# Splitting the direct f tiles into open, close and other halves, with eight single PSUM banks, in a gated bilinear feed-forward kernel on one Trainium2 core

## The chip, the cores and the metric

The kernel runs on one core of a Trainium2 chip. A core has five engines that run side by side, each with a queue of its own in order: TensorE (PE in the profile; PEld is its weight load), VectorE (DVE), ScalarE (ACT), GpSimd (POOL) and SyncE (SP), which issues most DMAs. TensorE writes to PSUM, which has eight banks of 128 x 512 fp32; the other data lie in SBUF. The metric is the device time of one execution in microseconds, median of several runs.

## The reference

What is computed, cut to what matters here (2048 rows, width 512, F = 1376):

```python
sa, ca, ga, sb, cb, gb = (mod[:, 0], mod[:, 1], mod[:, 2], mod[:, 3], mod[:, 4], mod[:, 5])
h = _layernorm(x, axis=-1) * (1 + ca) + sa
x = x + ga * _A_ref(h, A_wq, A_wk, A_wv, A_wo, A_beta)   # 32 heads, 4 segments, memory
h = _layernorm(x, axis=-1) * (1 + cb) + sb
x = x + gb * _B_ref(h, B_w_gate, B_w_up, B_w_down)
...
g = jnp.einsum("bsd,df->bsf", x, w_gate)
u = jnp.einsum("bsd,df->bsf", x, w_up)
h = g * u
return jnp.einsum("bsf,fd->bsd", h, w_down)
```

The change concerns only the last part, from the second layernorm on.

## The kernel before

Up to about 520 us the kernel does the attention and the product with wo. Behind it stands the gated feed-forward part. The 2048 rows are four segments of 512, taken as two pairs (p = 0: segments 0 and 1, p = 1: segments 2 and 3; c is the segment within its pair). F is cut into 11 tiles of 128 columns, the last (LAST, tile 10) with 96.

Every fp32 operand is held as a high and a low piece in the format fp32r, and a product is three matmuls (high x high, low x high, high x low). `six` (L1244) issues the six matmuls of one 256-deep product. Two f tiles and two segments are multiplied together by a scheme with seven products instead of eight, whose operands are sums and differences. A `unit` (L1352) is one such scheme for the gate (g) or the up (u) weights of two f tiles: products Z, Y, X in three PSUM banks, with copies to SBUF by ScalarE (`out_of`: p5, p1, y) and sums by VectorE (`add`, L1343). Its last two products (`seven`, `four`) are run inside the next unit. A pair of units (gate, then up) gives the mids of two f tiles: `finish` (L1328) multiplies gate and up (L1339) on VectorE where up lies in PSUM and on GpSimd otherwise, and `split` (L1269) makes the pieces mH (ScalarE) and mL (VectorE).

`build` (L1206) makes the pieces of the activations: for the combined operands GpSimd forms differences (b12 - b11 and so on) in the tile t (L1221), ScalarE makes the high piece bH (L1213) and VectorE the remainder bL (L1214). It is a generator: at each `next(nb)` one step is issued.

`down` (L1302) multiplies the mids of one or two f tiles with the down weights dH, dL, three matmuls for each, into a bank from `dbank` (L1258), and VectorE adds it to the row block xa (L1314). The banks of `dbank` rotate over lq0, the first half of lk, lq1 and the second half of lk, where lk is one tile of two banks.

Of pair p = 0 the f tiles 0, 1 and LAST are plain: `direct` (L1400) forms them without the scheme. For c = 0 there are an opening product (piece 1; its result is copied to q by ScalarE, L1413) and a closing product (piece 2) in the same bank; for c = 1 there are two products Y, to which q is added. Before: open and close of tile 0; four transposes of the layernorm (`run(lg1)`); open and close of tile 1; open and close of LAST; the down products of c = 0 (tiles 0 and 1 together, four row blocks; then LAST, four); then the c = 1 products of LAST, 0 and 1. The down products of c = 1 for these tiles are put off in the list dq: eight down products, four of LAST and four of tiles 0 and 1. Of dq the main loop (`d()`) takes one at given steps of each unit; before, three are in unit 0 and five in unit 1.

The down weights of the plain tiles, dHp and dLp, lie in the slot (wh1, wl1) in which the weight pieces cwH and cwL of unit 2 are made later, so unit 2's pieces wait for the last product that reads dHp and dLp. Weights of a unit are fetched two units ahead by `prepare`: a DMA on the SP queue into cr, sums cs on GpSimd (L478 to L482), high pieces by ScalarE (L486), low ones by GpSimd (L487). For p = 1 the pieces are fetched from DRAM instead, where p = 0 has kept them.

The order of TensorE is the order of the program (`pe`). The other engines' orders are settled when the program is built, by a scheduler that simulates the engines; `pin` only binds an instruction behind the last matmul issued, in that order, without a wait on the chip.

Of the kernel before, what the change touches and what calls it, by code (L numbers as in the profile page):

```python
# [17 lines left out]
P = 128  # L18
# [39 lines left out]
def tile_kernel(ctx, tc, x, wq, wk_, wv, wo, beta, w_gate, w_up, w_down, c, w_mod, out):  # L58
# [8 lines left out]
    def close(p):  # L67
        p.__exit__(None, None, None)
# [27 lines left out]
    TAGS = {"lq0": ("lq0", 1), "lq1": ("lq1", 1), "lk": ("lk", 1), "tb": ("tb", 1), "ms0": ("ms0", 1), "ms1": ("ms1", 1), "sm": ("sm", 1)}  # L96

    def pst(shape, tag, name, dt=F32):
        tg, n = TAGS[tag]
        return psp.tile(list(shape), dt, tag=tg, name=name, bufs=n)  # L100

    nbank, nlast = [0], [0]
    btag = ["ms", "tb", "ms", "sm"]
# [1099 lines left out]
    def tmp(name):  # L1203
        return pc.tile([P, L], F32, tag="t", name=name, bufs=NT)

    def build(p):  # L1206

        def emit(j, srcs):
            pool = bc if j < 3 else pc
            hi = pool.tile([P, 2, L], F32R, tag=f"bh{j}", name=f"bH{p}_{j}", bufs=1)  # L1210
            lo = pool.tile([P, 2, L], F32R, tag=f"bl{j}", name=f"bL{p}_{j}", bufs=1)
            for k in range(2):
                act.activation(hi[:, k], srcs[k], AF.Copy)  # L1213
                vec.tensor_sub(lo[:, k], srcs[k], hi[:, k].bitcast(F32))  # L1214
            pieces[p, j] = hi, lo

        T = pc.tile([P, 2, L], F32, tag="ws1", name=f"t{p}", bufs=1)

        def comb(a, b):
            for k in range(2):  # L1220
                nc.gpsimd.tensor_sub(T[:, k], a[k], b[k])  # L1221
            return t
# [12 lines left out]
        emit(6, comb(b22, t))  # L1235
        yield
        emit(4, comb(b21, t))
        yield
        emit(7, comb(b22, b12))
        yield  # L1240

    WI = {1: 4, 2: 5, 3: 3, 4: 6, 5: 0, 6: 1, 7: 2}
# [6 lines left out]
                pe(nc.tensor.matmul(ps[0:n], a, b[:, k], start=first and c == 0, stop=last and c == 5, skip_group_check=True))  # L1249
                c += 1  # L1250

    nx, nd, dq, lkt = [0], [0], [], [None]

    def xbank(name):
        nx[0] ^= 1
        return pst((P, 512), f"ms{nx[0]}", name)

    def dbank(name):  # L1258
        i = nd[0] % 4
        nd[0] += 1  # L1260
        if i % 2 == 0:
            return pst((P, 512), f"lq{i // 2}", name)
        if i == 1:
            lkt[0] = psp.tile([P, 2, 512], F32, tag="lk", name=name, bufs=1)
        return lkt[0][:, i // 2]

    mids, wds, x1a = {}, {}, {}

# [52 lines left out]
    def d(k=1):  # L1321
        for _ in range(k):
            if dq:
                dq.pop(0)()
# [3 lines left out]
    def finish(p, nm, f, c, v, psum):  # L1328

        n = ft[f][1]  # L1330
        if nm == "g":
            if psum:
                r = tmp(f"gs{p}_{f}_{c}")
                act.activation(r[0:n], v[0:n], AF.Copy)
                v = r
            gs[p, f, c] = v
            return
        g = gs.pop((p, f, c))
        (vec if psum else nc.gpsimd).tensor_mul(g[0:n], g[0:n], v[0:n])  # L1339
        split(p, f, c, g)  # L1340

    def add(a, b, n=P):
# [5 lines left out]
    def prev(k):  # L1348
        if len(tail) > k:
            tail[k]()  # L1350
# [46 lines left out]

        tail.extend((seven, four))

    def direct(p, f, c, qs=None):  # L1400

        n = ft[f][1]

        def mm(ps, nm, r, j, first, last):
            six(ps, *plain[p, f, nm], lambda k: (2 * r + k,), n, *pieces[p, j], first, last)

        if c == 0:
            Xs = [dirbank(f"X{nm}{p}_{f}") for nm in "gu"]
            qs = qs or [tmp(f"q{nm}{p}_{f}") for nm in "gu"]
            qt[p, f] = qs  # L1410
            for X, q, nm in zip(Xs, qs, "gu"):
                mm(X, nm, 0, 1, True, True)
                act.activation(q[0:n], X[0:n], AF.Copy)  # L1413
                yield 1
            for X, nm in zip(Xs, "gu"):
                mm(X, nm, 1, 2, False, True)
                finish(p, nm, f, 0, X, True)
                yield 2
            return
        for q, nm in zip(qt[p, f], "gu"):  # L1420
            Y = dirbank(f"Y{nm}{p}_{f}")
            mm(Y, nm, 0, 5, True, False)
            yield 3
            mm(Y, nm, 1, 3, False, True)
            finish(p, nm, f, 1, add(Y, q, n), False)
            yield 4

    qt = {}
    DB = ["ms0", "ms1", "tb", "sm"]
    ndir = [2]  # L1430

    def dirbank(name):
        ndir[0] += 1
        return pst((P, 512), DB[(ndir[0] - 1) % 4], name)

    def x_unit(n):

        for st in direct(1, LAST, 0):
            yield st
            if st == 1:  # L1440
                prev(0)
                tail[0:1] = []
        for st in direct(1, LAST, 1):
            yield st
        dq.extend(lambda c=c, t=t: down(1, (LAST,), c, t) for c in (0, 1) for t in range(4))

    def prepare(n):
# [73 lines left out]
    for n in range(NU):  # L1521
        p, nm, i = units[n]
        pr = prepare(n + 2)
        if p == 0:
            keep((nm, i), [a.rearrange("p a b c -> p (a b c)") for a in wslot[n]], wkeep)
        if n == CH - 1:
            nb = build(1)
        for st in (unit if nm != "x" else x_unit)(n):
            next(pr, None)
            if n == 0:  # L1530
                next(pr1, None)
                next(nb, None)
# [12 lines left out]
    d(99)  # L1545
    close(pcpool)
    close(wppool)
    close(B["bcpool"])
# [26 lines left out]
```

## Time and profile before

| | |
|---|---|
| median of 3 runs | 898.79 us (897.49 to 901.04) |
| the profiled execution | 899.35 us |
| its span, first to last instruction | 897.6 us |
| mean granted TensorE clock | 0.990 of full speed |
| TensorE busy after 720 us, stretch 720 to 760 | 37.88 of 40 us |
| VectorE, ScalarE, GpSimd busy in the whole span | 623.5, 496.3, 426.8 us |

The profile is of one execution. A row of a timeline has the start in microseconds, the duration, the engine, the line of the kernel, the operation, output and inputs, and in brackets how long the engine stood idle before it and what released it. The view of the waits adds these up by line and releaser. The view by stretches has for each engine the busy time with the count of instructions, and PEclk, the clock that the throttle granted. A share of busy time is an average over stages with different limits, so the stretches matter more than the page.

### The profile page before, as it was taken

The numbers are of one execution on the slowest core, as the hardware profiler recorded it, in microseconds if no ns is written. First come the engines' busy times: TensorE is split into PE (matmuls) and PEld (weight loads), VectorE is DVE, ScalarE is ACT, GpSimd is POOL, SyncE is SP. The second block draws the span as 40 slices with busy tenths as digits, with TensorE's granted clock in tenths as the row PEclk, the third lists the DMA queues.
The fourth block names the chain that finished last, engine by engine and source line by source line (L and its number), as shares of the span: only waits on it lengthen the run. The fifth ranks groups of instructions, "written<-read, shape, count | busy, mean of one in ns | idle before, by whom it ended". The sixth has DMA issues, their size and how long they took to land.

```text
span 897.6 us, 14464 instructions
## 1 busy us (share of the span) xinstructions
PE 855.1 (95%) x4976; PEld 600.3 (67%) x4976; DVE 623.5 (69%) x1689; ACT 496.3 (55%) x745; POOL 426.8 (48%) x552
## 2 busy tenths in 40 slices
PE   8989999989999999999999978999999999999998
PEld 4755656556565556666666766777788768888876
DVE  7798777888788877878887366775756834444444
ACT  3758767687676865777454452333444734554420
POOL 4546536565564763756235456638771401116310
PEclk9999999999999999999999999999999999999999
DMA  7555434454554555365674474447753565443012
GB/s 235 146 160 144 115 109 135 149 150 133 132 125 142 145 151 136 109 193 168 193 223 131 153 271 166 164 138 267 264 172 133 214 208 199 177 156 119 30 47 94
DMA packets 83305, 141.29 MB, mean 157 GB/s; under 512 B 11712, under 2 KB 45504, under 8 KB 83232
## 3 DMA queue, kind: packets, MB, share of 16 engines
q1 hardware_dynamic: 83088, 140.35, 49.6%
q8 instruction: 39, 0.64, 0.3%
q14 instruction: 34, 0.28, 0.1%
q10 hardware_dynamic: 144, 0.02, 0.0%
HBM read 90.52 MB, written 49.55 MB: 156 GB/s over the span
## 4 chain that ended last, share of the span: by engine, by line
PE 72%; DVE 14%; ACT 6%; POOL 3%; DMA 2%; issue 2%; SPq 0%; POOLq 0%; ACTq 0%; DVEq 0%
PE acc L1311 12%; PE tb L85 7%; PE q L85 6%; PE k L85 6%; PE Xg L1249 6%; PE Xu L1249 6%; DVE q L39 5%; PE wops L85 4%; PE vps L85 4%; PE Yu L1249 3%; PE kps L85 3%; PE Yg L1249 3%; PE qps L85 3%; ACT pt L331 2%; PE Zu L1249 1%
## 5 line engine op out<-in xcount | busy, mean ns | idle before, releaser
L39 DVE CUSTOM_DVE_ANT_0 q<-q,cmask 128x384 f32<-128x384 f32 (+3 forms) x512 | 246.5, 508 | 49.7 <-PE q L85 39.6
L331 ACT ACTIVATE pt<-k 128x1024 f32<-128x1024 f32 x160 | 163.8, 1024 | 64.4 <-PE k L85 63.7
L337 POOL TENSOR_SCALAR_AFFINE_SELECT pt<-pt 128x256 f32<-128x256 f32 (+1 forms) x224 | 96.8, 446 | 166.8 <-ACT pt L331 163.1
L85 PE MATMUL q<-kst,qst 96*128 96x384 bf16 (+3 forms) x512 | 101.5, 299 | 11.4 <-DVE nm L39 9.8
L1314 DVE TENSOR_TENSOR xa<-xa,acc 128x512 f32<-128x512 f32 x95 | 64.9, 683 | 62.2 <-PE acc L1311 62.0
L85 PE MATMUL k<-qst,kst 98*128 98x384 bf16 (+3 forms) x512 | 97.1, 302 | 5.0 <-ACT pt L331 4.9
L85 PE MATMUL tb<-pt,v 128*32 128x512 f32 (+3 forms) x1024 | 75.5, 436 | 0.0
L39 DVE DVE_READ_ACCUMULATOR2_ANT nm<- 128x1 f32 x512 | 72.0, 141 | 0.0
L85 PEld LDWEIGHTS <-kst 98*128 98x128 bf16 x512 | 37.7, 98 | 49.5 <-issue 43.2
L85 PEld LDWEIGHTS <-qst 96*128 96x128 bf16 x512 | 43.1, 97 | 37.9 <-issue 14.0
L1311 PE MATMUL acc<-dH,mH 128*128 128x512 f32 (+1 forms) x150 | 60.1, 401 | 0.0
L1311 PE MATMUL acc<-dH,mL 128*128 128x512 f32 (+1 forms) x150 | 59.6, 398 | 0.3 <-DVE mL L1274 0.3
L1311 PE MATMUL acc<-dL,mH 128*128 128x512 f32 (+1 forms) x150 | 59.7, 398 | 0.0
L1339 POOL TENSOR_TENSOR p1g<-p1g,p1u 128x512 f32<-128x512 f32 x9 | 11.7, 1295 | 95.1 <-DVE p1u L1343 95.1
L85 PEld LDWEIGHTS tb<-pt,v 128*32 128x32 f32 x1024 | 28.7, 109 | 38.6 <-issue 34.1
L363 ACT ACTIVATE tsb<-tb 128x512 f32<-128x512 f32 x32 | 19.0, 595 | 41.0 <-PE tb L85 41.0
L1311 PEld LDWEIGHTS acc<-dH,mL 128*128 128x128 f32 (+1 forms) x150 | 28.4, 190 | 7.3 <-DVE mL L1274 0.6
L1311 PEld LDWEIGHTS acc<-dH,mH 128*128 128x128 f32 (+1 forms) x150 | 28.4, 190 | 7.2 <-ACT mH L1273 0.3
L1311 PEld LDWEIGHTS acc<-dL,mH 128*128 128x128 f32 (+1 forms) x150 | 28.5, 190 | 7.1
L85 PE MATMUL kps<-ahH,wkH 128*128 128x512 f32 x64 | 29.7, 464 | 0.6 <-DVE ahH L39 0.6
L85 PE MATMUL wops<-woH,oH 128*128 128x512 f32 x64 | 28.3, 442 | 0.7 <-ACT oH L512 0.7
L85 PE MATMUL qps<-ahH,wqH 128*128 128x512 f32 x64 | 28.7, 448 | 0.0
(384 smaller groups left out, 2174.3 us busy)
## 6 DMA issues: line engine op xcount, KB each, us to landing
wm<-in_w_mod_dram SPq DMA_DIRECT2D x24, 256.0 KB, 4.9
kd<-k SPq DMA_DIRECT2D x16, 384.0 KB, 2.5
kst<-kd SPq DMA_DIRECT2D x32, 192.0 KB, 3.2
qd<-q SPq DMA_DIRECT2D x16, 384.0 KB, 2.9
qst<-qd SPq DMA_DIRECT2D x32, 192.0 KB, 3.6
x<-in_x_dram SPq DMA_DIRECT2D x16, 256.0 KB, 4.6
kst<-kd SPq DMA_DIRECT2D x32, 128.0 KB, 3.1
qst<-qd SPq DMA_DIRECT2D x32, 128.0 KB, 3.6
```

Source lines behind the costliest of these rows:

```text
L39: i = getattr(self.eng, name)(*a, **k)
L85: return pe(nc.tensor.matmul(*a, **k))
L331: ex = act.activation(pt, kp, AF.Exp, scale=0.25)
L337: sels[u, i] = nc.gpsimd.affine_select(w, w, pattern=[[0, w.shape[1]], [1, P]], compare_op=ALU.is_ge, fill=0.0, base=0, channel_multiplier=-1)
L363: act.activation(tsbs[u], tbs.pop(u), AF.Copy)
L1249: pe(nc.tensor.matmul(ps[0:n], a, b[:, k], start=first and c == 0, stop=last and c == 5, skip_group_check=True))
L1311: pe(nc.tensor.matmul(ps, a[0:m, t * P:(t + 1) * P], b[0:m], start=j == 0, stop=j == n - 1))
L1314: vec.tensor_add(xa, xa, ps)
L1339: (vec if psum else nc.gpsimd).tensor_mul(g[0:n], g[0:n], v[0:n])
```

## The change

- The PSUM pool of the first part is closed after it, and a second pool with eight single banks is opened; lk becomes lk0 and lk1, and `dbank` rotates over lk0, lq1, lk1 and lq0.
- `direct` is divided into `open0`, `close0` and `other`. The order is now: open of tiles 0 and 1, close of tile 0, the transposes, close of tile 1, open of LAST, two down products of tiles 0 and 1, close of LAST, two more; then `other(LAST)`, two down products of LAST, `other(0)`, the two others, `other(1)`.
- In `build` the differences on GpSimd and the splits are steps of their own, the splits are pinned, and for p = 1 the order of the steps differs. In the last units of p = 0 a step is issued at every step of the unit.
- In `finish` the multiplication is always on VectorE: 31 instructions, in both pairs, leave GpSimd.
- All eight put-off down products of c = 1 are issued in unit 0.

```diff
-    psp = ctx.enter_context(tc.tile_pool(name="psp", bufs=1, space=PSUM))
+    psppool, psp = open_pool(name="psp", bufs=1, space=PSUM)
+    PS = [psp]
...
+    close(psppool)
+    psgpool, PS[0] = open_pool(name="psg", bufs=1, space=PSUM, reuse_waits="tile")
...
             for k in range(2):
-                act.activation(hi[:, k], srcs[k], AF.Copy)
-                vec.tensor_sub(lo[:, k], srcs[k], hi[:, k].bitcast(F32))
+                pin(act.activation(hi[:, k], srcs[k], AF.Copy))
+                pin(vec.tensor_sub(lo[:, k], srcs[k], hi[:, k].bitcast(F32)))
...
         if p > 0:
+            emit(2, b21)
+            yield
+        comb(b12, b11)
+        yield
+        if p > 0:
             emit(1, b11)
             yield
-            emit(2, b21)
-            yield
-        emit(5, comb(b12, b11))
+        emit(5, t)
         yield
         emit(3, b22)
         yield
-        emit(6, comb(b22, t))
-        yield
+        comb(b22, t)
+        yield
+        emit(6, t)
+        yield
...
     def dbank(name):
-        i = nd[0] % 4
         nd[0] += 1
-        if i % 2 == 0:
-            return pst((P, 512), f"lq{i // 2}", name)
-        if i == 1:
-            lkt[0] = psp.tile([P, 2, 512], F32, tag="lk", name=name, bufs=1)
-        return lkt[0][:, i // 2]
+        return pst((P, 512), ("lq0", "lk0", "lq1", "lk1")[nd[0] % 4], name)
...
-        (vec if psum else nc.gpsimd).tensor_mul(g[0:n], g[0:n], v[0:n])
+        vec.tensor_mul(g[0:n], g[0:n], v[0:n])
...
+    def dmm(p, f, ps, nm, r, j, first, last):
+        six(ps, *plain[p, f, nm], lambda k: (2 * r + k,), ft[f][1], *pieces[p, j], first, last)
+
+    def open0(p, f, qs=None):
+
+        n = ft[f][1]
+        qt[p, f] = qs or [tmp(f"q{nm}{p}_{f}") for nm in "gu"]
+        xt0[p, f] = [dirbank(f"X{nm}{p}_{f}") for nm in "gu"]
+        for X, q, nm in zip(xt0[p, f], qt[p, f], "gu"):
+            dmm(p, f, X, nm, 0, 1, True, True)
+            act.activation(q[0:n], X[0:n], AF.Copy)
+            yield 1
+
+    def close0(p, f):
+
+        for X, nm in zip(xt0.pop((p, f)), "gu"):
+            dmm(p, f, X, nm, 1, 2, False, True)
+            finish(p, nm, f, 0, X, True)
+            yield 2
...
-    run(direct(0, 0, 0, qa[0]))
+    run(open0(0, 0, qa[0]))
+    run(open0(0, 1, qa[1]))
     next(xp)
+    run(close0(0, 0))
     run(lg1)
     nb = build(0)
     next(nb)
-    run(direct(0, 1, 0, qa[1]))
+    run(close0(0, 1))
     for w in wdp[:2]:
         next(w)
+    run(open0(0, LAST, qa[LAST]))
+    next(wdp[2])
     next(nb)
     next(pr0)
-    run(direct(0, LAST, 0, qa[LAST]))
-    next(wdp[2])
-    for t in range(4):
+    for t in range(2):
+        down(0, (0, 1), 0, t)
+    next(nb)
+    run(close0(0, LAST))
+    next(nb)
+    for t in range(2, 4):
         next(pr0, None)
         down(0, (0, 1), 0, t)
...
-    for t in range(4):
-        down(0, (LAST,), 0, t)
...
-    for f in (LAST, 0, 1):
-        for _ in direct(0, f, 1):
-            if f != LAST:
-                next(pr1, None)
-        if f == LAST:
-            next(nb)
+    run(other(0, LAST))
+    next(nb)
+    next(nb)
+    for f in (0, 1):
+        for t in (2 * f, 2 * f + 1):
+            down(0, (LAST,), 0, t)
+        for _ in other(0, f):
+            next(pr1, None)
+        next(nb)
...
-            if st in DS[nm] and n < NU - 1:
+            if n == 0:
+                d(1 + st % 2 if st > 1 else 1)
+            elif st in DS[nm] and n < NU - 1:
                 d()
             if 1 <= n < CH - 1:
                 next(lg, None)
-            if n == CH - 1 and st in (1, 3, 5, 6) or n == CH:
+            if n in (CH - 1, CH):
                 next(nb, None)
```

More of the change, by code (lines that the diff above doesn't have):

```diff
@@ L94, in tile_kernel @@
     dram = ctx.enter_context(tc.tile_pool(name="dram", bufs=1, space=DRAM))
-    psp = ctx.enter_context(tc.tile_pool(name="psp", bufs=1, space=PSUM))
-    TAGS = {"lq0": ("lq0", 1), "lq1": ("lq1", 1), "lk": ("lk", 1), "tb": ("tb", 1), "ms0": ("ms0", 1), "ms1": ("ms1", 1), "sm": ("sm", 1)}
+    psppool, psp = open_pool(name="psp", bufs=1, space=PSUM)
+    PS = [psp]
+    TAGS = {"lq0": ("lq0", 1), "lq1": ("lq1", 1), "lk": ("lk", 1), "lk0": ("lk0", 1), "lk1": ("lk1", 1), "tb": ("tb", 1), "ms0": ("ms0", 1), "ms1": ("ms1", 1), "sm": ("sm", 1)}
     def pst(shape, tag, name, dt=F32):
         tg, n = TAGS[tag]
-        return psp.tile(list(shape), dt, tag=tg, name=name, bufs=n)
+        return PS[0].tile(list(shape), dt, tag=tg, name=name, bufs=n)
     nbank, nlast = [0], [0]
@@ L1221, in comb @@
                 nc.gpsimd.tensor_sub(T[:, k], a[k], b[k])
-            return t
         t = [T[:, k] for k in range(2)]
@@ L1234, in build @@
         yield
-        emit(6, comb(b22, t))
+        comb(b22, t)
         yield
-        emit(4, comb(b21, t))
+        emit(6, t)
         yield
-        emit(7, comb(b22, b12))
+        comb(b21, t)
+        yield
+        emit(4, t)
+        yield
+        comb(b22, b12)
+        yield
+        emit(7, t)
         yield
@@ L1250, in six @@
                 c += 1
-    nx, nd, dq, lkt = [0], [0], [], [None]
+    nx, nd, dq = [0], [0], []
     def xbank(name):
@@ L1398, in unit, with other @@
         tail.extend((seven, four))
-    def direct(p, f, c, qs=None):
+    def dmm(p, f, ps, nm, r, j, first, last):
+        six(ps, *plain[p, f, nm], lambda k: (2 * r + k,), ft[f][1], *pieces[p, j], first, last)
+    def open0(p, f, qs=None):
         n = ft[f][1]
[L1404 to L1419, printed above, removed]
+        qt[p, f] = qs or [tmp(f"q{nm}{p}_{f}") for nm in "gu"]
[9 more added lines that the diff above has]
+            yield 2
+    def other(p, f):
+        n = ft[f][1]
         for q, nm in zip(qt[p, f], "gu"):
             Y = dirbank(f"Y{nm}{p}_{f}")
-            mm(Y, nm, 0, 5, True, False)
+            dmm(p, f, Y, nm, 0, 5, True, False)
             yield 3
-            mm(Y, nm, 1, 3, False, True)
+            dmm(p, f, Y, nm, 1, 3, False, True)
             finish(p, nm, f, 1, add(Y, q, n), False)
             yield 4
+    xt0 = {}
     qt = {}
@@ L1436, in x_unit @@
     def x_unit(n):
-        for st in direct(1, LAST, 0):
+        for st in open0(1, LAST):
             yield st
[L1440 to L1444, printed above, removed]
+            prev(0)
+            tail[0:1] = []
+        yield from close0(1, LAST)
+        yield from other(1, LAST)
         dq.extend(lambda c=c, t=t: down(1, (LAST,), c, t) for c in (0, 1) for t in range(4))
@@ L1545, in tile_kernel @@
     d(99)
+    close(psgpool)
     close(pcpool)
```

## The prediction

> **What bounds the kernel now.** I read the page first, then the waits of TensorE in the part that the diff touches (520.4 us to the end), then the timeline around each of these waits.
>
> ```profile
> span 897.6 us, 14464 instructions
> PE 855.1 (95%) x4976; PEld 600.3 (67%) x4976; DVE 623.5 (69%) x1689; ACT 496.3 (55%) x745; POOL 426.8 (48%) x552
> PE 72%; DVE 14%; ACT 6%; POOL 3%; DMA 2%; issue 2%; SPq 0%; POOLq 0%; ACTq 0%; DVEq 0%
> ```
>
> TensorE (PE) is busy for 95% of the span and carries 72% of the chain that ended last; the diff leaves out no matmul. A gain can only be time in which PE stands still or runs slowly, a loss only a new wait of PE. These are its waits after 520.4 us (total, times, longest):
>
> ```profile
> PE Xg L1249 <- ACT q L1413: 5.4, 2, 2.7
> PE Yg L1249 <- ACT p5g L1363: 3.9, 2, 2.1
> PE Zg L1249 <- POOL cwL L487: 2.3, 1, 2.3
> ...
> PE acc L1311 <- DVE mL L1274: 0.3, 1, 0.3
> ```
>
> The timeline of PE gives their places (start, duration; the wait in brackets):
>
> ```profile
> 528.68 0.66 PE L88 MATMUL ctp<-ident,x 128*128 128x128 f32 x4 [1.29 <-ACT chf L596]
> 534.81 0.50 PE L1249 MATMUL Xg<-bh,gH 128*128 128x512 f32 x1 [2.73 <-ACT q L1413]
> 535.40 0.63 PE L1249 MATMUL Xg<-bl,gH 128*128 128x512 f32 x1
> 535.83 0.63 PE L1249 MATMUL Xg<-bh,gH 128*128 128x512 f32 x1
> ...
> 544.92 0.48 PE L1249 MATMUL Xg<-bh,cwH-1_6808 128*96 128x512 f32 x1 [2.70 <-ACT q L1413]
> ...
> 555.30 0.39 PE L1311 MATMUL acc<-dLp,mH 96*128 96x512 f32 x1
> 555.78 0.50 PE L1311 MATMUL acc<-dHp,mH 96*128 96x512 f32 x1
> ...
> 582.11 0.50 PE L1249 MATMUL Yg<-bH,cwH 128*128 128x512 f32 x1 [1.75 <-ACT p5g L1363]
> ...
> 604.38 0.49 PE L1249 MATMUL Zg<-bh,cwH 128*128 128x512 f32 x1 [0.49 <-ACT cwH L486]
> 607.17 0.79 PE L1249 MATMUL Zg<-bh,cwL 128*128 128x512 f32 x1 [2.29 <-POOL cwL L487]
> 617.74 0.39 PE L1311 MATMUL acc<-dH,mL 128*128 128x512 f32 x1
> ...
> 732.28 0.50 PE L1249 MATMUL Yg<-bH,cwH 128*128 128x512 f32 x1 [2.12 <-ACT p5g L1363]
> ```
>
> Granted clock by stretches (length; busy time and count of PE, PEld, DVE, ACT, POOL; PEclk; DMA):
>
> ```profile
> 528.00:535.00 7.00, 3.58 (x17) 2.76 (x18) 5.54 (x5) 6.37 (x12) 7.00 (x5) 1.00 1.04 369
> 535.00:545.00 10.00, 7.30 (x25) 5.13 (x24) 9.91 (x9) 4.70 (x9) 9.37 (x8) 0.83 0.36 134
> 600.00:617.00 17.00, 14.22 (x55) 11.05 (x54) 13.10 (x17) 7.10 (x13) 14.58 (x16) 0.90 0.54 201
> 617.00:650.00 33.00, 33.00 (x152) 26.64 (x150) 21.78 (x32) 14.53 (x25) 25.94 (x27) 1.00 0.78 279
> ```
>
> Without waits a matmul takes 33.00/152 = 0.22 us. After a long gap the starts lie 0.43 us apart (535.40 to 535.83), and the clock of that stretch is 0.83 or 0.90. In the timeline some 8 matmuls go so after each gap of 1.75 us and more: 8 x 0.21, about 1.6 us on top of the gap. After the gap of 1.29 us the stretch shows 1.00, so I charge none there.
>
> The Trainium skill (TensorE: Matmul & The Clock Gate, Why this matters for your kernels) advises against idle gaps above some 3 us. By it, gaps of 1.75 to 2.73 us would not have slowed the clock, and removing them would save the gaps alone; this trace has slow matmuls after each, so I go by the trace.
>
> **What is removed.** (1) The closing products of f tile 1 and of the last tile wait for the copy of their own opening products. In the new order another tile's products lie between: 2.73 + 2.70, and 1.6 after each, 8.6 us. (2) The 1.29 at the transposes is given to the same reordering; the last tile's down products lose two waits for a half of the two-bank tile (555.30 to 555.78 is 0.48, 0.25 over the usual distance; the second alike). Together 1.8. (3) In unit 0, Yg waits for p5g because ScalarE stands at mH, whose product GpSimd makes late:
>
> ```profile
> 580.42 0.63 ACT L1273 ACTIVATE mH<-q 128x512 fp32r<-128x512 f32 x1 [1.74 <-POOL q L1339]
> 581.48 0.58 ACT L1363 ACTIVATE p5g<-Yg 128x512 f32<-128x512 f32 x1
> ```
>
> Now that mul is on VectorE, and four held-back down products stand between Yg's halves: 1.75 + 1.6 = 3.4. (4) Unit 2's weights lie in the slot of the held-back down weights, which is free at the end of unit 0 instead of unit 1, so Zg finds its pieces: 0.49 + 2.29 + 1.6 = 4.4. Sum: 8.6 + 1.8 + 3.4 + 4.4 = 18.2.
>
> **What is added, at the first down product.** It needs mL of f tile 1. PE gets there so: from 534.81 take the waits 2.73 and 1.29, add 24 matmuls (closing f tile 1, opening the last tile), 536.1, and its second half about 0.7 later; say 537.0. In the built program's order ScalarE has the first copy of b12-b11 ahead of mH, VectorE its remainder ahead of mL, and GpSimd makes that difference only after cwL-1 and five instructions for the next unit's weights (three cs, two cwL):
>
> ```profile
> 526.91 2.79 POOL L435 TENSOR_TENSOR cwL-1_6809<-cr-1_6810,cwH-1_6808 128x1024 fp32r<-128x1024 f32 x1 [16.09 <-ACT cwH-1_6808 L434]
> 529.66 1.74 POOL L1221 TENSOR_TENSOR t<-chf,chf 128x512 f32<-128x512 f32 x1
> 531.36 1.18 POOL L478 TENSOR_TENSOR cs<-cr 128x256 f32<-128x256 f32 x1
> ...
> 535.32 1.73 POOL L487 TENSOR_TENSOR cwL<-cr,cwH 128x512 fp32r<-128x512 f32 x1
> ...
> 558.10 0.73 POOL L478 TENSOR_TENSOR cs<-cr 128x256 f32<-128x256 f32 x1 [7.86 <-DMA cr<-in_w_up_dram]
> ...
> 564.75 1.30 POOL L487 TENSOR_TENSOR cwL<-cr,cwH 128x512 fp32r<-128x512 f32 x1 [3.71 <-ACT cwH L486]
> ```
>
> ```profile
> 531.08 0.94 ACT L486 ACTIVATE cwH<-cr 128x512 fp32r<-128x512 f32 x2 [0.17 <-DMA cr<-in_w_gate_dram]
> 540.41 1.77 DVE L1214 TENSOR_TENSOR bL<-t,bH 128x512 fp32r<-128x512 f32 x1
> 542.70 0.68 DVE L1214 TENSOR_TENSOR bL<-t,bH 128x512 fp32r<-128x512 f32 x1
> ```
>
> The weights cr land at 531.0. Then GpSimd needs, at the short durations, 3 x 0.73 + 1.30 + 0.73 and 1.29 for the difference (by L487 of the same size): ready at 536.5. At the long ones, 3 x 1.18 + 1.73 + 1.18 + 1.74: 539.2. Behind it come the copy (0.6), one remainder at 1.77 and one at 0.68: mL at 539.5 to 542.5. PE waits 2.5 to 5.5 and pays the slow clock, 1.6: bounds 2.5 (without it) and 7.1. The stretch 535 to 545 had VectorE at 9.91 and GpSimd at 9.37 of 10, so I go toward the upper end: 5.8. Behind the stopped down product stand only PE's own products.
>
> **What is added, at the first down product of pair one (f tiles 2, 3; c = 1).** Before, it came 108 matmuls after the start of Zu of unit 1; now 81, since 27 of the held-back products are ahead. PE's cover shrinks by 27 x 0.22 = 5.9 us while VectorE gains three muls in it:
>
> ```profile
> 601.81 1.28 DVE L1289 TENSOR_TENSOR crd<-crd,gbb 128x512 f32<-128x512 f32 x2
> 611.50 0.69 DVE L1343 TENSOR_TENSOR p5u<-Xu,p5u 128x512 f32<-128x512 f32 x1 [2.96 <-PE Xu L1249]
> 612.10 2.86 DVE L587 TENSOR_SCALAR x<-x,cmv,cy 128x512 f32<-128x512 f32 x3
> 615.50 0.68 DVE L1274 TENSOR_TENSOR mL<-p5g,mH 128x512 fp32r<-128x512 f32 x1
> ```
>
> From p5u to the matmul that needs mL there are 617.74 - 611.50 = 6.2 us. By the new order eleven VectorE instructions lie there: four x at 0.95 (2.86 for three) and seven others at 0.6 (611.50 to 612.10): 8.0. That is a wait of 1.8, if no more is contended. At the far end the four with two inputs in SBUF take 1.8 instead of 0.68 (the 1.77 above), 4.3 more, and the slow clock 1.6: 7.7. The nearest rows, 601.81 to 615.50, show short durations, so I take the short wait with its slow stretch: 3.4.
>
> **At no cost.** Of the 31 muls taken from GpSimd the others stand in units where PE was always busy:
>
> ```profile
> L1339 DVE TENSOR_TENSOR gs<-gs,Xu x13: 671/678/689, 526.2 to 872.3; 128x512 f32<-128x512 f32 x11, 96x512 f32<-96x512 f32 x2
> L1339 POOL TENSOR_TENSOR p5g<-p5g,p5u x9: 1288/1292/1522, 612.3 to 869.4; 128x512 f32<-128x512 f32 x9
> ```
>
> One takes 0.68 instead of 1.29, so what follows it comes earlier unless VectorE is late; it had 11 us free of 33 in the stretch from 617. If that cover fails, rival C. The single banks add no wait; the wait at 732.28 for p5g (2.12, behind a fetched weight copy) keeps its order and stays, as does the tail.
>
> On this the Trainium skill (SBUF — State Buffer, Who interferes with whom) speaks against the change: a VectorE instruction with two SBUF inputs and a GpSimd one that reads SBUF block each other. The trace agrees that something does: 1.77 against 0.68 for the same line.
>
> Sum: -18.2 + 5.8 + 3.4 = -9.0. The profiled execution took 899.35 us (span 897.6), 0.56 above the median of 898.79. So 898.8 - 9.0 = **889.8 us**. With both added waits at their low ends (2.5, 1.8) it is 884.9, at their high ends 895.4.
>
> **Rivals.** A: no new waits, because mL comes in time at both places: 880.6. For it: the short GpSimd durations at 558. Against: the order puts the difference behind five instructions. B: both at full price, 895.4. For it: GpSimd busy for all of 528 to 535. C, slower: VectorE becomes last at the end of later pairs. PE already waits once for mL (0.3), so a delay of VectorE there shows at once. GpSimd is busy for 25.94 of 33 us in the stretch from 617; I take three pairs at such a load. Each such wait at 3 us (the size of the ones now removed) with 1.6 is 4.6; three of them and B: 895.4 + 13.8 = 909. It decides for slower from the second full wait on. Against: clock 1.00 and PE busy throughout from 617 to 650. D: the change doesn't do what it says: p5g and Zg still wait, their releaser being a fetch rather than the mul or slot: 889.8 + 3.4 + 4.4 = 897.6. By the skill's rule on gaps the slow stretches are in neither sum: -11.8 + 4.2 + 1.8 = -5.8, 893.0, which I give 0.05.
>
> **How the numbers follow.** My forecast (884.9 to 894) has 0.49, A 0.14, B 0.14, C 0.13, D 0.05, the rule 0.05. A measurement of this kernel can tell about 0.5%, 4.5 us, from no change: the forecast, A and the rule are faster (0.68), B and D the same (0.19), C slower (0.13). The range goes from A, 880.0, past D to 900.0: what is left out is C and little below A.
>
> **What would show it.** Right: no gap above 1 us in closing products; Zg of unit 2 and Yg of unit 0 without a wait; one wait of PE at the first down product for mL, one at the first of pair one; no mul of L1339's kind on GpSimd; VectorE about 20 us busier. Wrong: waits for mL in later pairs (C), no wait in the two new places (A), Yg or Zg still waiting (D), or a clock below 1.00 where PE has no gap.

## The result, and the profile after

The changed kernel takes 901.27 us (median of 20 runs, 899.39 to 903.71); the kernel before took 898.72 beside it. The ratio is 1.0033 with a 95% interval of 1.0022 to 1.0045: 2.5 us slower, where 889.8 had been forecast. The two profiled executions, 899.35 before and 900.34 after, lie 1.0 us apart, and the account below is made between these two.

TensorE's waits in the changed kernel from 520 us on (total, times, longest):

```profile
PE Xu L1260 <- DVE p5u L1349: 5.2, 3, 2.8
PE acc L1317 <- ACT mH L1279: 5.1, 2, 3.0
PE acc L1317 <- DVE mL L1280: 4.4, 2, 3.1
PE Yg L1260 <- ACT p5g L1369: 2.4, 1, 2.4
PE Xu L1260 <- DVE yu L1349: 1.2, 2, 0.9
...
```

Every wait that was to go is gone: none of the closing products, of Yg in unit 0 or of Zg in unit 2. In their place stand waits for mH and mL, forecast as one wait for mL at each of two places, and for p5u, which were not forecast. Their places, in TensorE's timeline of the changed kernel:

```profile
521.10 0.50 PE L1260 MATMUL Xg<-bh,gH 128*128 128x512 f32 x1 [0.78 <-DVE xr L39]
...
539.61 0.49 PE L1317 MATMUL acc<-dHp,mH 128*128 128x512 f32 x1 [2.11 <-ACT mH L1279]
541.35 0.50 PE L1317 MATMUL acc<-dHp,mL 128*128 128x512 f32 x1 [1.24 <-DVE mL L1280]
...
594.73 0.40 PE L1260 MATMUL Zg<-bh,cwH 128*128 128x512 f32 x1
...
604.71 0.40 PE L1317 MATMUL acc<-dH,mH 128*128 128x512 f32 x1
...
608.56 0.50 PE L1317 MATMUL acc<-dH,mH 128*128 128x512 f32 x1 [2.98 <-ACT mH L1279]
612.19 0.79 PE L1317 MATMUL acc<-dH,mL 128*128 128x512 f32 x1 [3.13 <-DVE mL L1280]
618.54 0.48 PE L1260 MATMUL Zu<-bh,cwH 128*128 128x512 f32 x1
...
646.34 0.50 PE L1260 MATMUL Xu<-bH,cwH 128*128 128x512 f32 x1 [2.81 <-DVE p5u L1349]
...
711.29 0.50 PE L1260 MATMUL Xu<-bH,cwH 128*128 128x512 f32 x1 [1.62 <-DVE p5u L1349]
...
734.79 0.50 PE L1260 MATMUL Yg<-bH,cwH 128*128 128x512 f32 x1 [2.38 <-ACT p5g L1369]
...
894.32 0.40 PE L1317 MATMUL acc<-dL,mH 128*128 128x512 f32 x1
```

And the same matmuls in the kernel before, as far as they are not shown above:

```profile
520.45 0.39 PE L1249 MATMUL Xg<-bh,gH 128*128 128x512 f32 x1
...
616.80 0.40 PE L1311 MATMUL acc<-dH,mH 128*128 128x512 f32 x1
...
621.77 0.48 PE L1249 MATMUL Zu<-bh,cwH 128*128 128x512 f32 x1
...
893.38 0.40 PE L1311 MATMUL acc<-dL,mH 128*128 128x512 f32 x1
```

The reader should subtract row from row. The part begins 0.65 us late (521.10 against 520.45). At Zg of unit 2 the changed kernel is 9.65 us ahead (594.73 against 604.38), and as Zg no longer waits, 12.09 ahead at the first matmul of pair one's first down product (604.71 against 616.80). At Zu of unit 3, right behind the next ones, it is 3.23 ahead (618.54 against 621.77): 8.9 us are gone there. The wait at 646.34 with its slow stretch takes the rest and 0.6 more, the one at 711.29 adds 1.62, and at the last matmul the changed kernel is 0.94 behind (894.32 against 893.38). The stretches show where the clock fell:

```profile
535.00:545.00 10.00, 6.65 (x22) 4.45 (x21) 8.72 (x9) 6.33 (x11) 9.38 (x8) 0.84 0.59 208
600.00:617.00 17.00, 10.10 (x34) 7.34 (x33) 14.18 (x16) 6.13 (x10) 13.26 (x13) 0.80 0.66 240
617.00:650.00 33.00, 30.19 (x131) 23.95 (x130) 23.33 (x35) 12.84 (x22) 11.12 (x13) 0.96 0.44 152
720.00:760.00 40.00, 37.62 (x163) 29.84 (x162) 17.44 (x27) 16.54 (x26) 0.00 (x0) 1.00 0.66 225
```

From 600 to 617 us TensorE ran 34 matmuls where the kernel before ran 55. What VectorE and GpSimd did there, in the changed kernel:

```profile
597.70 2.89 DVE L1295 TENSOR_TENSOR crd<-crd,gbb 128x512 f32<-128x512 f32 x1
...
601.11 0.68 DVE L1349 TENSOR_TENSOR p5u<-Xu,p5u 128x512 f32<-128x512 f32 x1
...
603.46 3.26 DVE L588 TENSOR_SCALAR x<-x,cmv,cy 128x512 f32<-128x512 f32 x3
606.63 1.21 DVE L1345 TENSOR_TENSOR p5g<-p5g,p5u 128x512 f32<-128x512 f32 x1
607.76 2.58 DVE L588 TENSOR_SCALAR x<-x,cmv,cy 128x512 f32<-128x512 f32 x1
...
611.46 0.68 DVE L1280 TENSOR_TENSOR mL<-p5g,mH 128x512 fp32r<-128x512 f32 x1
```

```profile
597.19 2.85 POOL L488 TENSOR_TENSOR cwL<-cs,cwH 128x1024 fp32r<-128x1024 f32 x1
...
607.26 2.80 POOL L488 TENSOR_TENSOR cwL<-cs,cwH 128x1024 fp32r<-128x1024 f32 x1
```

The mL that TensorE waits for (611.46) stands behind four scalings x of the next layernorm. Two of VectorE's instructions last as long as a weight piece of GpSimd that runs at the same time: crd ends at 600.59 and cwL at 600.04, x at 610.34 and cwL at 610.06.

### The profile page after: what moved, and what is told of

Read it like the earlier page. It is cut to its first block, busy times and chain, and to the rows that moved or that the text cites. A ratio compares the mean times of both kernels' runs of the same rounds, so it can differ in the third digit from the quotient of the medians.

```text
span 898.6 us, 14447 instructions
## 1 busy us (share of the span) xinstructions
PE 852.6 (95%) x4975; PEld 600.1 (67%) x4976; DVE 647.0 (72%) x1720; ACT 496.7 (55%) x745; POOL 389.3 (43%) x521
## 4 chain that ended last, share of the span: by engine, by line
PE 71%; DVE 15%; ACT 6%; DMA 2%; issue 2%; POOL 2%; SPq 1%; ACTq 0%; DVEq 0%; POOLq 0%
PE acc L1317 13%; PE tb L85 7%; PE q L85 6%; PE k L85 6%; PE Xg L1260 6%; DVE q L39 5%; PE Xu L1260 5%; PE wops L85 4%; PE vps L85 4%; PE Yg L1260 4%; PE Yu L1260 4%; PE kps L85 3%; PE qps L85 2%; ACT pt L332 2%; PE Zu L1260 1%
## 5 line engine op out<-in xcount | busy, mean ns | idle before, releaser
L479 POOL TENSOR_TENSOR cs<-cr 128x256 f32<-128x256 f32 x10 | 8.6, 856 | 107.2 <-DMA cr<-in_w_gate_dram 102.3
L488 POOL TENSOR_TENSOR cwL<-cr,cwH 128x512 fp32r<-128x512 f32 (+1 forms) x20 | 22.7, 1158 | 40.9 <-ACT cwH L487 40.9
L1260 PE MATMUL Xu<-bH,cwH 128*128 128x512 f32 (+1 forms) x68 | 27.4, 403 | 6.4 <-DVE p5u L1349 5.2
```

The lines of the kernel that those rows point to most:

```text
L479: gp.tensor_add(S[:, 0], A(1, 0), A(1, 1))
L488: gp.tensor_sub(wl[:, d], v, wh[:, d].bitcast(F32))
```

## The experiments

The names used in the expectations: M says that the gate times up products fill VectorE by themselves; Q, that it is what stands ahead of the last mL in VectorE's queue; P, that it is the cover taken out of unit 1; L, that VectorE stands still for whole GpSimd instructions; W says that the wait at the first down product hangs on the place that the difference b12 - b11 has on GpSimd, A that mL of tile 1 comes at its own time whatever GpSimd does (this A is not the prediction's rival A). Every run was timed in five rounds beside the kernel before; ratios are to that kernel, with a 95% interval. Versions that lie within some 2 us of each other have overlapping intervals; between these the text goes by the traces.

| run | median us | ratio | interval |
|---|---|---|---|
| products back on GpSimd | 893.77 | 0.9944 | 0.9923 to 0.9966 |
| put-off products spread | 894.69 | 0.9951 | 0.9934 to 0.9968 |
| scalings x four steps later | 889.26 | 0.9890 | 0.9865 to 0.9915 |
| weight pieces in quarters | 897.25 | 0.9976 | 0.9961 to 0.9992 |
| x later, difference first | 888.72 | 0.9892 | 0.9873 to 0.9911 |
| before, products on VectorE alone | 895.66 | 0.9974 | 0.9958 to 0.9989 |
| x later, difference first, products shared | 886.32 | 0.9860 | 0.9838 to 0.9883 |
| before, put-off products in unit 0 alone | 903.54 | 1.0056 | 1.0035 to 1.0078 |
| shared, last tile closed first | 885.48 | 0.9841 | 0.9818 to 0.9864 |
| the same, weight work free | 884.49 | 0.9834 | 0.9812 to 0.9857 |
| before, put-off and single banks | 900.22 | 1.0014 | 0.9994 to 1.0034 |
| x later, all products on GpSimd | 887.24 | 0.9864 | 0.9842 to 0.9885 |

### Products back on GpSimd

```diff
-        vec.tensor_mul(g[0:n], g[0:n], v[0:n])
+        (vec if psum else nc.gpsimd).tensor_mul(g[0:n], g[0:n], v[0:n])
```

> The changed kernel with one part undone: the gate times up products that come from SBUF are on GpSimd again. In the changed kernel TensorE loses 9.9 us at the first down product of pair one (waits 2.98 for mH and 3.13 for mL, then the slow clock), and 2.81 and 1.62 to p5u at 646 and 711 us. Theory M (the moved products themselves fill VectorE): both go, the wait at pair one falls under 1 us and no p5u wait is left: about 901.3 - 9.9 - 4.4 = 887. Theory Q (the queue in front of the last product counts: scalings x of the next layernorm stand ahead of mL on VectorE and are held up by GpSimd's weight pieces of 2.3 to 2.9 us): the p5u waits go, but at pair one the product now stands behind these weight pieces on GpSimd, and 3 us or more of wait stay: 891 to 897.

It took 893.77. Pair one still waits. Of the p5u waits the one of 2.81 shrinks to 0.31, and those of 0.79 and 1.62 go (0.17 stands at 752.36, where the changed kernel has none). The scalings x on VectorE, and TensorE's waits, of this run:

```profile
603.83 4.04 DVE L588 TENSOR_SCALAR x<-x,cmv,cy 128x512 f32<-128x512 f32 x4
```

```profile
609.12 0.79 PE L1317 MATMUL acc<-dH,mL 128*128 128x512 f32 x1 [3.46 <-DVE mL L1280]
...
640.17 0.50 PE L1260 MATMUL Xu<-bH,cwH 128*128 128x512 f32 x1 [0.31 <-DVE p5u L1349]
```

With no product on VectorE, four x still stand ahead of mL. So M is out for pair one, and right for the p5u waits of 2.81 and 1.62: in the changed kernel's order these need the products on VectorE.

### Put-off products spread over units 0 and 1

```diff
-            if n == 0:
-                d(1 + st % 2 if st > 1 else 1)
-            elif st in DS[nm] and n < NU - 1:
+            if st in DS[nm] and n < NU - 1:
                 d()
```

> The changed kernel with one part undone: the put-off down products of c = 1 are three in unit 0 and five in unit 1 again. Theory P (the loss at pair one comes from the 27 matmuls of cover taken out of unit 1): the waits of 6.1 us there fall under 1 us, and what comes back is the wait of Zg for unit 2's weights, 2.8 us and a slow stretch: 901.3 - 9.9 + 4.4 = 896, or lower. Theory Q: the cover of 5.9 us hides most of the 6.1 as well, so both agree on that place; by Q the p5u waits at 646 and 711 (2.81, 1.62) stay, by P, if all the loss comes from the earlier arrival of TensorE, they shrink by the time given back.

It took 894.69. No wait is left at pair one; Zg waits again, 0.49 and 1.21, and Yg 0.61 behind it, for the weight pieces. The cover is a condition of the loss, with one thing that comes with it: the slot of unit 2's weights is again free late, GpSimd's large piece starts at 609.16, behind that mL (607.68), and the four x take 3.4 (0.96, 1.93 and 0.53). Which of the two counts for more this run does not part. But the wait for p5u is the same 2.81 as in the changed kernel, though TensorE now reaches it some 5 us earlier:

```profile
641.05 0.50 PE L1260 MATMUL Xu<-bH,cwH 128*128 128x512 f32 x1 [2.81 <-DVE p5u L1349]
```

So that wait is no matter of how early TensorE comes; VectorE's chain moves with it.

### Scalings x four steps later

```diff
-            if 1 <= n < CH - 1:
+            if 1 <= n < CH - 1 and (n > 1 or st > 4):
                 next(lg, None)
```

> The changed kernel with the steps of the next layernorms (loads, statistics, scalings x, transposes) begun four steps later, so that on VectorE no scaling x stands ahead of the product p5g and of mL at the first down product of pair one. Nothing else changes. Theory Q: mL comes some 6 us earlier (three x 3.26 and one x 2.58 leave the queue), the wait at pair one falls from 6.1 to under 1.5 us, and the p5u wait at 646 us, where an x that waits 0.94 for GpSimd stands ahead, falls from 2.81 to under 1: about 889 to 893. Theory M: the same time as the changed kernel within 2 us, because the products themselves are what is late.

It took 889.26, 12.0 us less than the changed kernel with the same products, banks and order of TensorE's work, except that the transposes come later too. VectorE begins the mL that TensorE waits for at 607.57 instead of 611.46. At pair one TensorE waits 1.34 for p5u and 0.51 for mL, instead of 0.79 for p5u and 6.1 for mH and mL, and at the end of the next pair not at all. Q holds at both places.

### Weight pieces in quarters

```diff
         for d, v in ((slice(4, 6), top), (6, A(1, 1)), (slice(0, 4), S)):
             act.activation(wh[:, d], v, AF.Copy)
-            gp.tensor_sub(wl[:, d], v, wh[:, d].bitcast(F32))
+            if d == slice(0, 4):
+                for j in range(4):
+                    gp.tensor_sub(wl[:, j], S[:, j], wh[:, j].bitcast(F32))
+            else:
+                gp.tensor_sub(wl[:, d], v, wh[:, d].bitcast(F32))
```

> The changed kernel with the longest weight-piece subtraction of each unit on GpSimd (128 x 1024, 2.4 to 2.9 us) issued as four of 128 x 256. GpSimd's total work is the same or a little more. Theory L (VectorE's instructions with two inputs in SBUF, and the scalings x, stand still for a whole GpSimd instruction): the 2.89 of crd at 597.70 and the 2.58 of x at 607.76 fall to 1.3 or less, and the wait at pair one falls from 6.1 to 3 or 4 us: 895 to 898. If they share the port in turn all along, the durations add up to the same and the time stays within 1.5 us of 901.3.

It took 897.25. VectorE in this run:

```profile
597.91 1.23 DVE L1299 TENSOR_TENSOR crd<-crd,gbb 128x512 f32<-128x512 f32 x1
...
604.02 3.54 DVE L592 TENSOR_SCALAR x<-x,cmv,cy 128x512 f32<-128x512 f32 x4 [0.80 <-POOL cy L589]
```

The crd that took 2.89 takes 1.23, beside a piece of GpSimd of 1.19, and four x take 3.54 where three and one took 3.26 and 2.58. Shorter instructions of GpSimd hold VectorE up for less, as L says; by the rival, sharing in turn, the time would have stayed within 1.5 us of 901.3. TensorE still waits 4.42 for mL, where L had 3 to 4: the queue is the greater part.

### The kernel before with one part of the change

The first has the products on VectorE alone, the second all put-off products in unit 0 alone, the third the second with the eight single banks.

```diff
-        (vec if psum else nc.gpsimd).tensor_mul(g[0:n], g[0:n], v[0:n])
+        vec.tensor_mul(g[0:n], g[0:n], v[0:n])
```

> The kernel before with the gate times up products on VectorE alone, nothing else of the change. Theory Q (VectorE's chain up to p5u does not get earlier when TensorE does; before, p5u was done 0.3 us ahead of TensorE at 646): the 1.75 for p5g in unit 0 goes, Zg's wait for unit 2's weights stays (it hangs on the slot), TensorE comes to p5u at 646 and 711 earlier or VectorE later, and waits 1 to 3 us at each: 898 to 902. Theory M (VectorE with three products more in each pair is the bound by itself): a wait for mL at pair one of 2 us or more beside them: 903 or more.

It took 895.66, better than either theory had it. It has no wait at pair one, and one p5u wait:

```profile
645.52 0.50 PE L1249 MATMUL Xu<-bH,cwH 128*128 128x512 f32 x1 [2.81 <-DVE p5u L1343]
```

Again 2.81. By itself this part is a gain of 3.1 us: p5g's wait in unit 0 falls to 0.84 and Zg's second wait to 1.20.

```diff
-            if st in DS[nm] and n < NU - 1:
+            if n == 0:
+                d(1 + st % 2 if st > 1 else 1)
+            elif st in DS[nm] and n < NU - 1:
                 d()
```

> The kernel before with all eight put-off down products of c = 1 in unit 0, nothing else of the change: the products gate times up stay on GpSimd. Theory P and Q agree that Zg's wait (0.49 + 2.29 and a slow stretch, 4.4) goes. By P (the cover of 27 matmuls is what pair one lacks, whatever engine multiplies) a wait of 3 to 6 us with a slow stretch comes at the first down product of pair one: 897 to 902. By M (the products on VectorE are what is late) no wait comes there: 894.5.

It took 903.54: alone, this part is a loss of 4.8 us. Pair one waits 1.07 and 3.46, the same as with the changed kernel's products back on GpSimd. A wait that no theory had named stands in unit 0. TensorE of this run:

```profile
585.67 0.80 PE L1311 MATMUL acc<-dHp,mH 96*128 96x512 f32 x1 [4.38 <-DVE xa L1314]
```

And with the single banks too:

```diff
+    close(psppool)
+    psgpool, PS[0] = open_pool(name="psg", bufs=1, space=PSUM, reuse_waits="tile")
...
-        i = nd[0] % 4
         nd[0] += 1
-        if i % 2 == 0:
-            return pst((P, 512), f"lq{i // 2}", name)
-        if i == 1:
-            lkt[0] = psp.tile([P, 2, 512], F32, tag="lk", name=name, bufs=1)
-        return lkt[0][:, i // 2]
+        return pst((P, 512), ("lq0", "lk0", "lq1", "lk1")[nd[0] % 4], name)
```

> The kernel before with all eight put-off down products in unit 0, as in the earlier run of that part alone, which took 903.5, and with the eight single banks of the change in addition. There TensorE waited 4.38 at the second put-off product for an xa of VectorE. If that wait is for the bank (half of the two-bank tile is still read by xa), it goes with its slow stretch: 897 to 899.5, and the loss at pair one (1.07 + 3.46 and a slow stretch, products on GpSimd) stays. If VectorE is simply late there, the wait stays and the time is within 1.5 us of 903.5.

With the banks it took 900.22, 3.3 us less; the upper end of the expectation was 899.5. The wait of 4.38 is gone, though the sums xa of VectorE come as late (584.94 without the banks, 586.17 with them), so it was for the two-bank tile. It stood at the fourth put-off product, the last one of LAST, and not at the second, as the expectation says; a wait of 0.99 for xa stands at the sixth, of tiles 0 and 1 (586.90). Pair one's wait stays (3.45).

### The wait at the first down product

```diff
+        wpin = pin if n == 0 else (lambda i: i)
-        gp.tensor_add(S[:, 0], A(1, 0), A(1, 1))
+        wpin(gp.tensor_add(S[:, 0], A(1, 0), A(1, 1)))
...
-            gp.tensor_sub(wl[:, d], v, wh[:, d].bitcast(F32))
+            wpin(gp.tensor_sub(wl[:, d], v, wh[:, d].bitcast(F32)))
```

> The run before it with the scalings x begun four steps later, and with one step more: the weight sums and low pieces of unit 0 are bound behind the opening product of the last tile, so that on GpSimd the difference b12 - b11 stands right behind cwL-1 and ahead of them. Theory W (the wait at the first down product, 2.50 + 1.23 with a slow stretch, some 5 us, comes from that difference standing behind five weight instructions): the difference is made from 533.7 on, as soon as its operand is there, mL comes at 537 to 538.5, the wait falls to 1.5 or less: 884 to 887. Rival (ScalarE and VectorE are as late for reasons of their own, their copies and remainders): the wait stays at 2.5 or more and the time at 888 to 890.

This is made from the run with x later. It took 888.72, 0.5 less than without this step. GpSimd makes the difference from 533.12 on and ScalarE has copied both halves at 537.62, and still TensorE waits 1.28 for mH and 1.72 for mL, where it was 2.50 and 1.23. ScalarE's copies, then VectorE, then TensorE, of this run:

```profile
535.98 0.60 ACT L1341 ACTIVATE gs<-Xg 128x512 f32<-128x512 f32 x1
...
538.03 0.63 ACT L1280 ACTIVATE mH<-gs 128x512 fp32r<-128x512 f32 x1
```

```profile
534.93 1.31 DVE L1281 TENSOR_TENSOR mL<-gs,mH 128x512 fp32r<-128x512 f32 x1 [1.65 <-ACT mH L1280]
536.16 1.23 DVE L1298 TENSOR_TENSOR dLp<-crd,dHp 128x512 fp32r<-128x512 f32 x1
537.32 0.68 DVE L1346 TENSOR_TENSOR gs<-gs,Xu 128x512 f32<-128x512 f32 x1
...
539.12 1.75 DVE L1281 TENSOR_TENSOR mL<-gs,mH 128x512 fp32r<-128x512 f32 x1
```

```profile
540.93 0.79 PE L1318 MATMUL acc<-dHp,mL 128*128 128x512 f32 x1 [1.72 <-DVE mL L1281]
```

The product gs of tile 1 itself comes at 537.32: ScalarE has copied its gate only at 536.58, and VectorE, which stood 1.65 for tile 0's mH, does that tile's mL and a weight remainder ahead of it. W, which had a wait of 1.5 or less, falls. The difference is not without a part, though. In the changed kernel ScalarE stands 1.34 for it, and mH of tile 1, whose product has been there since 537.84, is copied only behind it:

```profile
538.41 0.63 ACT L1216 ACTIVATE bH<-t 128x512 fp32r<-128x512 f32 x1 [1.34 <-POOL t L1224]
538.95 0.61 ACT L1279 ACTIVATE mH<-gs 128x512 fp32r<-128x512 f32 x1
```

With the difference first the wait for mH is 1.2 shorter; but its remainders are then ahead of mL on VectorE, and the wait for mL is 0.5 longer.

Closing the last tile before the first two down products gives TensorE 12 matmuls more there:

```diff
-    for t in range(2):
-        down(0, (0, 1), 0, t)
     next(nb)
     run(close0(0, LAST))
+    for t in range(2):
+        down(0, (0, 1), 0, t)
     next(nb)
```

> The kernel with the shared products (x later, difference first, products of tiles 8, 9 and of p = 1 on GpSimd), with one edit: the last tile is closed before the first two down products instead of after them. There TensorE waited 1.52 for mH and 1.73 for mL and then ran slowly. Theory A (mL of tile 1 comes at its own time, some 3 us after TensorE, whatever GpSimd does, so 12 matmuls more ahead of it, 2.7 us, hide it): the two waits fall to 1 us or less, but a wait of up to 0.7 for q of the last tile comes ahead of its closing product: 2 to 4 us less, 882 to 884.5. Rival (the closing product brings its own instructions on VectorE and ScalarE ahead of mL, which then comes later by as much): within 1 us of 886.3.

It took 885.48, 0.8 less than the run it was made from (that with the products shared, below). The waits for mH and mL are gone, and the wait for q of the last tile took their place, not 0.7 but 2.85, since ScalarE has four copies of the difference and of b22 ahead of it. By its time the run lies in the rival's range, but not for the rival's reason:

```profile
539.78 0.47 PE L1261 MATMUL Xg<-bh,cwH-1_6812 128*96 128x512 f32 x1 [2.85 <-ACT q L1417]
```

Without the binding of unit 0's weight work, all else the same:

> The run before it in this set without the binding of unit 0's weight work on GpSimd: the difference b12 - b11 again stands behind five weight instructions. By the order, mH of tile 1 then stands ahead of the second piece of the difference on ScalarE. Theory W (that place on GpSimd decides when mL comes): slower than the run before it by 1.5 us or more. Theory A (it does not): within 1 us of it.

It took 884.49, 1.0 less and not 1.5 more: with the difference late again, q comes ahead of its copies on ScalarE, and the wait is 1.27 and 0.32. The difference of 1.0 is not clear of noise, but 1.5 more is ruled out, and W falls a second time. This is the fastest version found: 1.7% under the kernel before, 16.8 us under the changed one.

### Sharing the products

```diff
-        vec.tensor_mul(g[0:n], g[0:n], v[0:n])
+        (nc.gpsimd if not psum and (p == 1 or f in (8, 9)) else vec).tensor_mul(g[0:n], g[0:n], v[0:n])
```

> The first run of this set with one edit: the gate times up products of f tiles 8 and 9 of pair p = 0 and of all of p = 1 are on GpSimd, which has little to do there, those of the other tiles on VectorE. By theory Q the p5u wait of 1.62 at the end of the pair of tiles 8 and 9 goes and no new one comes: 1.0 to 2.5 us less than the first run of the set. By theory M, where each product on VectorE is a delay, the time falls further, as the yu and p5g waits after 720 us go too: 3 us or more less.

The first run of that set is the one with x later and the difference first, 888.72. It took 886.32, 2.4 less: the p5u wait of 1.62 is gone, and so is one of 1.11 after 748 us.

> The run with x later and the difference first (888.7), with all products from SBUF back on GpSimd. Theory Q (the scalings x and the cover decide at pair one, the engine of the product only in second place): the wait at pair one is under 2 us here too, although the product now stands behind weight pieces of 2.4 us on GpSimd, and the p5u waits at the end of tiles 8 and 9 go: 886 to 889. Theory M (products on VectorE are the loss): 884 or less. If GpSimd's queue holds p5g back, the wait at pair one is 3 us or more: 890 or more.

With all of them on GpSimd it took 887.24, and the wait for mL at pair one is 0.26:

```profile
608.23 0.50 PE L1318 MATMUL acc<-dH,mL 128*128 128x512 f32 x1 [0.26 <-DVE mL L1281]
```

p5u waits 1.37 just ahead of it, as in the run with the products on VectorE, where mL waited 0.50. Once x is out of the way, pair one does not care which engine multiplies. M falls.

## Why the prediction was wrong, point by point

**What is removed: right.** The closing products' waits, p5g in unit 0 and both of Zg's waits went. The terms of the sum up to Zg give 8.6 + 1.8 + 3.4 - 5.8 and Zg's first wait of 0.49, 8.5 us ahead; measured 9.65, after a start that is 0.65 late. The 31 products have left GpSimd, and VectorE is busy for 647.0 us, 23.5 more, where about 20 had been forecast.

**The first down product: right in place and size, in cause only in part.** Waits of 2.11 and 1.24 and a slow stretch (clock 0.84) stand against 5.8 with bounds of 2.5 and 7.1 (the upper one is added up wrongly: 539.2 + 0.6 + 1.77 + 0.68 gives mL at 542.2 and 6.9). I had put it down to the difference behind five weight instructions of GpSimd. The difference holds up mH by about a microsecond, but the runs with it first and with the weights free again show that the time hardly hangs on this place: ScalarE and VectorE are late with the tile's own pieces.

**The first down product of pair one: the term that failed by its size.** Forecast 3.4, at most 7.7; measured 10.0: 8.9 in the down product itself (2.98 and 3.13 and a clock of 0.80), and 0.79 for p5u and 0.35 for yu just ahead of it. Of the 6.6 above the forecast 4.3 are the wait (6.1 and not 1.8), 1.2 its slow stretch (2.8 and not 1.6) and 1.1 the two small waits. The mechanism was the one named, 27 matmuls of cover less and a full queue on VectorE. What I mis-sized is that queue and the time it had. The eleven instructions from p5u to mL took 11.0 us (601.11 to 612.14) and not 8.0, the four x among them 5.8 and not 3.8. And p5u itself was late, so TensorE was ready for mL some 4.5 us after it began and not 6.2. I took the short durations of "the nearest rows", though the same step frees the slot of unit 2's weights 18.65 us earlier (its last reader starts at 584.85 instead of 603.50) and so brings GpSimd's weight pieces forward: the large one that lies beside x at 607.26 is the fifth made from cs after 540 us, and the fifth came at 625.24 before. A single x beside it took 2.58 and not 0.95. My upper bound has a wait of 6.1 too, but that is luck: it let four instructions with two inputs in SBUF grow to 1.8, of which none took more than 1.22, and not x, which has one. The experiments show the conditions: with the cover and the late pieces back there is no wait for mH or mL, with x out of the queue 0.51; with the products back on GpSimd it is still 4.9 us.

**At no cost: wrong.** The step named busy TensorE and free VectorE from 617 to 650 as cover. The rows that decide are VectorE's and TensorE's in the kernel before:

```profile
645.36 0.68 DVE L1343 TENSOR_TENSOR p5u<-Xu,p5u 128x512 f32<-128x512 f32 x1
```

```profile
646.38 0.39 PE L1249 MATMUL Xu<-bH,cwH 128*128 128x512 f32 x1
```

p5u was done at 646.04, 0.34 ahead of the matmul that needs its bank. A stretch with 11 us of free VectorE had 0.34 us to spare at that place. In the changed kernel a product, and an x that waits for GpSimd's cy, stand ahead of p5u:

```profile
639.65 0.68 DVE L1345 TENSOR_TENSOR yg<-yg,yu 128x512 f32<-128x512 f32 x1
641.27 0.94 DVE L588 TENSOR_SCALAR x<-x,cmv,cy 128x512 f32<-128x512 f32 x1 [0.94 <-POOL cy L585]
...
645.61 0.68 DVE L1349 TENSOR_TENSOR p5u<-Xu,p5u 128x512 f32<-128x512 f32 x1
```

The wait of 2.81 goes with either: 0.31 with the products back, none with x later. It was 2.81 also in the kernel before with the products alone. This is rival C in its place and its kind, VectorE last at the end of later pairs, but it holds back p5u, not mL, and at two ends of pairs and not three. The 1.62 at 711.29 goes when the products of tiles 8 and 9 are on GpSimd; it is not there in the kernel before with all products on VectorE, so something else of the change has a part in it. It is there too with the put-off products spread (1.61) and with x later (1.62), so neither of these is it. The mL ahead of p5u takes 1.83 at 708.20, beside a difference of GpSimd, and 0.69 in that kernel before; whether the new order of `build` brings this about was not tried.

**The single banks add no wait: wrong by little, and with all put-off products in unit 0 they are needed.** The part starts 0.65 later, behind a wait of 0.78 for xr that the kernel before has not and the run with the single banks has. In turn they take away the wait of 4.38 that the put-off products meet in unit 0 without them, and leave one of 0.99.

**The sum.** -18.2 + 5.8 + 3.4 = -9.0 was forecast. The removed part held; 6.6 more at pair one and 3.8 and 1.6 at the two p5u waits, 12 us in all, turn it into a loss of 3.1. The last matmul is only 0.94 behind: up to pair one the change had gained some 0.9 more than forecast, and after 711 us 1.3 came back, as the gap at 734.79 has no slow stretch. What came lies between my rivals B (895.4) and C (909, to which I gave 0.13): pair one is above its full price, and VectorE is last at the end of two later pairs.

## What to carry to other kernels

Free time of an engine over a stretch says nothing of a single wait; look, for each instruction that feeds the bottleneck, how long before its use it was done, and treat a few tenths as none. When a change frees a slot or a buffer earlier, list what starts earlier because of it, and price the instructions beside it at their contended durations. And look at what stands in the queue ahead of the last operand: here work of a later stage, whose issue four steps later was worth 12 us, while undoing either of the change's two costly parts gave 7.5 and 6.6.

## What the runs showed of the hardware

A long gap does not always slow the clock. These are stretches of the run with the last tile closed first (a gap of 2.85 at 539.78), of the kernel before (2.12 at 732.28) and of the run with x later (1.80 at 723.52):

```profile
535.00:545.00 10.00, 7.15 (x32) 5.04 (x31) 8.53 (x10) 6.33 (x12) 8.00 (x8) 1.00 0.86 290
```

```profile
729.00:745.00 16.00, 13.88 (x54) 10.83 (x53) 4.14 (x6) 5.59 (x8) 0.00 (x0) 0.89 0.63 220
```

```profile
720.00:730.00 10.00, 8.20 (x29) 6.26 (x28) 1.76 (x3) 5.04 (x7) 0.00 (x0) 0.83 0.68 235
```

The longest gap has no slow stretch, the shortest has one; nor has the gap of 2.38 at 734.79 in the changed kernel (720 to 760 at 1.00), which gave 1.6 us back that the kernel before had paid. The same wait for p5u, 2.81 at the end of the same pair, is followed by matmuls 0.43 us apart in the changed kernel (641 to 655 us at 0.88) and by none in the kernel before with the products on VectorE (1.00). My 1.6 after each gap of 1.75 and more came from the kernel before, where all five have it; it is no rule. The Trainium skill (TensorE: Matmul & The Clock Gate, Part 1: The HAM clock gate (the "warmup" mystery)) has the activity window run free, without starting anew with the work; like gaps with and without a slow stretch agree with that, though the window itself is in no trace here.

A scaling with one input in SBUF is held up by GpSimd as well: 2.58 beside a cwL of 2.80, 0.54 for a like one at 646.93 with GpSimd idle. The Trainium skill (SBUF — State Buffer, Who interferes with whom) names tensor_scalar among the operations that can enter modes with both ports, and has whoever issues first keep the shared ports for the whole instruction. The trace agrees: x ends at 610.34, 0.28 after cwL. Whether x ran in such a mode no trace here shows.
